# Second feed-forward product in halves of 256 columns, one PSUM bank each; both sums of the first product in one bank

## The chip, the cores and the metric

The kernel runs on one core of a Trainium2 chip. The metric is the device time of one execution in microseconds, median of several runs. The engines have one instruction queue each: TensorE (PE; its weight loads are listed apart as PEld), VectorE (DVE), ScalarE (ACT), GpSimd (POOL) and SyncE (SP, which issues the transfers). TensorE writes its results to PSUM, which has eight banks of 512 fp32 columns on 128 partitions; only ACT and DVE read them from there in this kernel.

## The reference

Windowed attention for 4 batches, 8 heads, 768 positions and a head width of 64, followed by a feed-forward layer on 3072 tokens of 512 values, with a hidden width of 2048:

```python
scores_l = scale * q @ k.T, kept where |i - j| < 16, else -1e9
scores_s = scale * q @ max_of_each_32_keys.T + log(32)
a = softmax(concat(scores_l, scores_s))
x = (a @ concat(v, mean_of_each_32_values))     # -> 3072 x 512 over all heads
h = x @ w_in                                    # 512 -> 2048
g = s * relu(h) ** 2 + b
return g @ w_out                                # 2048 -> 512, fp32
```

## The kernel before

The 3072 tokens are taken in 12 chunks `c` of `T = 256` tokens. For a chunk, attention runs in four units `p` of two heads, and leaves the chunk's `x` turned, 4 blocks `kc` of 128 values by 256 tokens. The feed-forward layer then goes over 16 blocks `f` of 128 hidden values.

- `hidden(c, f)` is the first product: tile `ph`, 128 hidden values by 256 tokens. From chunk 1 on, `x` and the weights are split in a rounded high part (`xh`, `wh`) and the rest (`xl`, `wl`), in the type fp32r, and three products of parts are summed: 3 terms by 4 blocks, 12 matmuls with 256 moving columns. Chunk 0 works in plain fp32 with 4 matmuls.
- `activate(c, f)` makes `g`: ACT takes relu out of PSUM (L371) and squares (L372), POOL multiplies and adds (L379), DVE rounds to `gh` (L381) and forms the rest `gl` (L383).
- `project(c, f)` is the second product: for each half `t` of the tokens, the three terms gl x wh, gh x wl, gh x wh with 512 moving columns of `w_out`, 6 matmuls (L398), summed over all 16 `f` in two tiles `po`.
- `evict(c)` copies the two `po` with ACT (L406) to SBUF and sends them out.

The order on each engine is written out by hand: `plan` holds functions under a step number, and they are called step by step, within a step by the order LOAD, SPLIT, ATT, WEIGHTS, HID, PE_ATT, CHAIN, PROJ, EVICT. Step `i = 16 c + f` has `activate(c, f)`. From chunk 1 on the matmuls go in pairs:

```python
at(i if c == 0 else i - i % 2, HID, hidden, c, f)
at(i, CHAIN, activate, c, f)
at(i + LAG if i + LAG < NF else (i + LAG) | 1, PROJ, project, c, f)
```

So TensorE's queue reads: hidden of an even and an odd block (24 matmuls), perhaps a piece of the next chunk's attention, project of the two blocks before (12 matmuls), and so on. The attention pieces are `transposes` (tile `pt`, four matmuls, turned probabilities), `values` (tile `pav`, 16 matmuls a unit) and `scores` (tiles `ps`, 16 matmuls a unit). From chunk 2 on, a chunk's hidden blocks 0 to 15 carry four `pt` pieces of one unit each, and two times `pav` and `ps` for two units together.

ACT's queue holds, between the two activations of a pair, what attention has for that step, and in chunk 1 also the roundings of the weights to `wh` (L143), two a step.

Eight PSUM banks are shared out by five pools: two for `po`, two for `ph`, two for `ps`, one for `pt`, one for `pav`. A framework puts a semaphore wait wherever an instruction writes or reads a tile that another engine still uses; two parts of one PSUM tile count as the same tile for this.

Of the kernel before, what the change touches and what calls it, by code (L numbers as in the profile page):

```python
# [10 lines left out]
F32 = mybir.dt.float32  # L11
# [7 lines left out]
P = 128  # L19
B, H, S, D = 4, 8, 768, 64  # L20
DM, DFF = 512, 2048
# [5 lines left out]
KR = WIN + NB  # L27
NSUB = 4
T = NSUB * SUB
# [5 lines left out]
NF = DFF // P  # L35
# [9 lines left out]
def windowed_attention_then_relu2_ffn(ctx, tc, qk, vwin, kt, vt, kq, vrow, wp, sb, out):  # L45


    nc = tc.nc
# [9 lines left out]
    ps_s = ctx.enter_context(tc.tile_pool(name="ps_s", bufs=2, space=bass.MemoryType.PSUM))  # L58
    ps_t = ctx.enter_context(tc.tile_pool(name="ps_t", bufs=1, space=bass.MemoryType.PSUM))
    ps_v = ctx.enter_context(tc.tile_pool(name="ps_v", bufs=1, space=bass.MemoryType.PSUM))  # L60

    ident = const.tile([P, P], F32, name="ident")
    sb_col = const.tile([P, 2], F32, name="sb_col")
# [132 lines left out]
    pm = []  # L196

    def mean_of_rows(n):
        if n == 0:
            pm.append(ps_po.tile([P, DM], F32, name="pm", tag="po"))  # L200
# [14 lines left out]
    qk_t, vw_t, ps_of, pr_of, mn_of, sm_of, pt_of, pT_of, o_of, xt = ({} for _ in range(10))  # L215
# [33 lines left out]
    def scores(c, p, j):  # L249
        q, kw = qk_t[c, p]  # L250
        if j == 0:
            if c == 0 and p % 2:
                both = [ps_h.tile([P, T], F32, name="ps", tag="ph") for _ in range(2)]
                ps_of[c, p] = [t[:, : 2 * KR].rearrange("p (j k) -> p j k", k=KR) for t in both]
            elif c < 2:
                ps_of[c, p] = [ps_s.tile([P, 4, KR], F32, name="ps", tag="ps") for _ in range(2)]
            elif p % 2 == 0:
                both = [ps_s.tile([P, 4, KR], F32, name="ps", tag="ps") for _ in range(2)]
                ps_of[c, p], ps_of[c, p + 1] = [t[:, :2] for t in both], [t[:, 2:] for t in both]
        for e in range(2):  # L260
            r = slice(64 * e, 64 * e + 64)
            for a in range(2):
                i = 2 * j + a
                o, qi = ps_of[c, p][e][64 * a : 64 * a + 64, j], q[r, i * SUB : (i + 1) * SUB]
                if c > 0:
                    nc.tensor.matmul(o, qi, kw[r, i, :], start=True, stop=True)  # L266
                    continue
                w = win_start(i)
                nc.tensor.matmul(o[:, :WIN], qi, kraw[0, p][r, w : w + WIN], start=True, stop=True)
                nc.tensor.matmul(o[:, WIN:], qi, ksum[0, p][r], start=True, stop=True)  # L270
# [38 lines left out]

    def transposes(c, p):  # L310
        pr = pr_of.pop((c, p))
        pt_of[c, p] = ps_t.tile([P, 4 * P], F32, name="pt")
        for n in range(4):
            nc.tensor.transpose(pt_of[c, p][:KR, n * P : (n + 1) * P], pr[:, n, :], ident)  # L314

# [7 lines left out]
    def values(c, p):  # L323
        vw, pT = vw_t.pop((c, p)), pT_of.pop((c, p))
        if c == 0 and p % 2:
            o_of[c, p] = ps_po.tile([P, DM], F32, name="pav", tag="po")
        elif c < 2 or p % 2 == 0:
            o_of[c, p] = ps_v.tile([P, 2 * T], F32, name="pav")
            if c > 1:
                o_of[c, p + 1] = o_of[c, p][:, T:]  # L330
        o = o_of[c, p]
        for i in range(NSUB):
            for e in range(2):
                nc.tensor.matmul(  # L334
                    o[64 * e : 64 * e + 64, i * SUB : (i + 1) * SUB],
                    vw[:, e, i, :], pT[:, e * T + i * SUB : e * T + (i + 1) * SUB], start=True, stop=True,
                )
# [11 lines left out]
            nc.vector.tensor_tensor(xt[c][1][:, kcs], o, xt[c][0][:, kcs].bitcast(F32), ALU.subtract)  # L349


    ph_of, gg, po = {}, {}, {}

    def hidden(c, f):
        ph = ph_of[c, f] = ps_h.tile([P, T], F32, name="ph", tag="ph")
        if c == 0:
            terms = [(w_f["in", f], xt[c][0], kc) for kc in range(NKC)]
        else:
            xh, xl = xt[c]
            terms = [  # L360
                (w["in", f], x, kc) for w, x in ((w_l, xh), (w_h, xl), (w_h, xh)) for kc in range(NKC)
            ]
        for n, (w, x, kc) in enumerate(terms):
            nc.tensor.matmul(  # L364
                ph, w[:, kc * P : (kc + 1) * P], x[:, kc], start=(n == 0), stop=(n == len(terms) - 1)
            )

    def activate(c, f):
        ph = ph_of.pop((c, f))
        r = p2.tile([P, T], F32, name="r")  # L370
        nc.scalar.activation(r, ph, AF.Relu)  # L371
        nc.scalar.activation(r, r, AF.Square)  # L372
        if c == 0:
            g = p2.tile([P, T], F32, name="g0", tag="gh", bufs=4)
            nc.vector.tensor_scalar(g, r, s_col, b_col, ALU.mult, ALU.add)  # L375
# [7 lines left out]
        nc.vector.tensor_tensor(gl, g, gh.bitcast(F32), ALU.subtract)  # L383
        gg[c, f] = gh, gl

    def project(c, f):
        if f == 0:
            for t in range(T // P):
                po[t] = ps_po.tile([P, DM], F32, name="po", tag="po")
        g = gg.pop((c, f))  # L390
        if c == 0:
            terms = [(g[0], w_f["out", f])]
        else:
            gh, gl = g
            terms = [(gl, w_h["out", f]), (gh, w_l["out", f]), (gh, w_h["out", f])]
        for t in range(T // P):
            for n, (a, w) in enumerate(terms):
                nc.tensor.matmul(  # L398
                    po[t], a[:, t * P : (t + 1) * P], w,
                    start=(f == 0 and n == 0), stop=(f == NF - 1 and n == len(terms) - 1),  # L400
                )

    def evict(c):
        for t in range(T // P):
            o = stage.tile([P, DM], F32, name="o", tag="stage")
            nc.scalar.copy(o, po[t])  # L406
# [86 lines left out]
    for i in range(NC * NF):  # L493
        c, f = divmod(i, NF)
# [65 lines left out]
```

## Time and profile before

| | us |
|---|---|
| median of 3 runs | 649.14 (648.83 to 649.5) |
| the profiled execution | 648.71 |
| its span in the profile | 647.0 |
| PE busy in the span | 628.1 (97%), 5164 matmuls and 5164 weight loads |
| DVE busy | 336.8 (52%) |
| ACT busy | 330.5 (51%) |
| POOL busy | 153.8 (24%) |
| mean granted TensorE clock | 0.999 |

How to read it: busy time counts overlapping matmuls once. The duration of a matmul row is modelled and longer than its share of the stream, since matmuls overlap, so the pace of TensorE is read from the starts of rows that follow each other, or from the chain of waits, which lists stretches of the critical engine one behind the other. A row "x24" in the chain is 24 instructions of that line. A row of the timeline begins with its start in us from the span's start and its length.

### The profile page before, as it was taken

How to read it: one execution, taken by the hardware profiler on the slowest of the kernel's cores; microseconds unless marked ns; L12 is line 12 of the kernel's file. 1: busy time of each engine (PE TensorE's matmuls, PEld its weight loads, DVE VectorE, ACT ScalarE, POOL GpSimd, SP SyncE). 2: the span in 40 equal slices, each digit the busy share in tenths (PEclk: the TensorE clock that was granted, in tenths of full speed). 3: DMA queues.
4: the chain of work that ended last, by engine and by line, in shares of the span. 5: the costliest groups of instructions: out<-in, count | busy, mean ns of one | idle time of the engine just before them, and what ended most of it. 6: DMA issues, size and time to landing. Idle time of an engine off the chain costs nothing.

```text
span 647.0 us, 13898 instructions
## 1 busy us (share of the span) xinstructions
PE 628.1 (97%) x5164; PEld 547.0 (85%) x5164; DVE 336.8 (52%) x1102; ACT 330.5 (51%) x972; POOL 153.8 (24%) x324
## 2 busy tenths in 40 slices
PE   6699999999999999999999999999999999999997
PEld 4456568989989899898999899898998989999996
DVE  6799998885443434356434434447443353342221
ACT  4898957845444435535435345444444444452322
POOL 3000004143133132232231331331322322312221
PEclk9999999999999999999999999999999999999999
DMA  9999405035203204134402301404410320100000
GB/s 329 388 382 352 128 2 186 2 102 191 72 1 104 72 2 131 57 82 145 138 1 62 115 2 36 152 22 135 145 65 2 105 72 2 57 3 1 33 2 33
DMA packets 25604, 63.25 MB, mean 98 GB/s; under 512 B 3968, under 2 KB 3968, under 8 KB 25536
## 3 DMA queue, kind: packets, MB, share of 16 engines
q1 hardware_dynamic: 25536, 62.36, 29.1%
q8 instruction: 41, 0.67, 0.4%
q14 instruction: 27, 0.22, 0.1%
HBM read 55.90 MB, written 6.29 MB: 96 GB/s over the span
## 4 chain that ended last, share of the span: by engine, by line
PE 86%; DVE 7%; DMA 5%; issue 0%; ACT 0%; SPq 0%; DVEq 0%
PE po L398 39%; PE ph L364 38%; PE pav L334 4%; PE ps L266 3%; PE pt L314 3%; DMA qk<-in_qk_dram 2%; DMA vw<-in_vwin_dram 1%; DMA wraw<-in_wp_dram 1%; DVE wf_out L134 1%; DVE wf_in L132 1%; DVE wf_out L132 1%; DMA kq<-in_kq_dram 1%; DVE wf_in L134 1%; DVE wf_in L130 1%; DVE wf_out L130 1%; DVE g L375 1%
## 5 line engine op out<-in xcount | busy, mean ns | idle before, releaser
L379 POOL TENSOR_SCALAR g<-r,sb_col 128x256 f32<-128x256 f32 x176 | 101.8, 578 | 418.5 <-ACT r L372 324.5
L381 DVE CAST gh<-g 128x256 fp32r<-128x256 f32 x176 | 52.3, 297 | 269.0 <-POOL g L379 268.6
L371 ACT ACTIVATE r<-ph 128x256 f32<-128x256 f32 x192 | 73.4, 382 | 210.1 <-PE ph L364 207.6
L398 PE MATMUL po<-wh,gl 128*128 128x512 f32 x352 | 143.2, 407 | 0.0
L398 PE MATMUL po<-wh,gh 128*128 128x512 f32 x352 | 138.6, 394 | 0.0
L398 PE MATMUL po<-wl_out,gh 128*128 128x512 f32 x352 | 137.7, 391 | 0.0
L364 PE MATMUL ph<-xh,wl_in 128*128 128x256 f32 x704 | 110.9, 280 | 0.0
L364 PE MATMUL ph<-xl,wh 128*128 128x256 f32 x704 | 108.7, 276 | 0.0
L364 PE MATMUL ph<-xh,wh 128*128 128x256 f32 x704 | 108.7, 276 | 0.0
L364 PEld LDWEIGHTS ph<-xh,wl_in 128*128 128x128 f32 x704 | 100.2, 188 | 8.2 <-issue 0.7
L364 PEld LDWEIGHTS ph<-xl,wh 128*128 128x128 f32 x704 | 93.8, 188 | 0.0
L364 PEld LDWEIGHTS ph<-xh,wh 128*128 128x128 f32 x704 | 92.9, 188 | 0.0
L372 ACT ACTIVATE r<-r 128x256 f32<-128x256 f32 x192 | 80.2, 418 | 6.1
L383 DVE TENSOR_TENSOR gl<-g,gh 128x256 fp32r<-128x256 f32 x176 | 76.4, 434 | 6.0
L398 PEld LDWEIGHTS po<-wh,gh 128*128 128x128 f32 x352 | 66.1, 188 | 14.3
L398 PEld LDWEIGHTS po<-wh,gl 128*128 128x128 f32 x352 | 66.2, 188 | 14.1 <-issue 3.0
L398 PEld LDWEIGHTS po<-wl_out,gh 128*128 128x128 f32 x352 | 66.3, 188 | 11.5
L298 ACT ACTIVATE pr<-pr,mn 128x120 f32<-128x120 f32 x176 | 67.3, 384 | 6.0 <-DVE mn L285 5.7
L321 ACT COPY pT<-pt 120x512 f32<-120x512 f32 x48 | 28.2, 587 | 35.8 <-PE pt L314 35.6
L364 PEld LDWEIGHTS ph<-x,wf_in 128*128 128x128 f32 x128 | 23.6, 190 | 17.3 <-issue 8.0
L244 POOL COPY vw<-vsum 24x256 f32<-24x256 f32 x80 | 36.7, 499 | 1.3
L364 PE MATMUL ph<-x,wf_in 128*128 128x256 f32 x128 | 31.0, 385 | 6.0 <-DVE wf_in L134 4.1
(70 smaller groups left out, 613.4 us busy)
## 6 DMA issues: line engine op xcount, KB each, us to landing
wraw<-in_wp_dram SPq DMA_DIRECT2D x32, 512.0 KB, 10.0
qk<-in_qk_dram SPq DMA_DIRECT2D x44, 368.0 KB, 4.7
vw<-in_vwin_dram SPq DMA_DIRECT2D x48, 192.0 KB, 4.6
out_dram<-o SPq DMA_DIRECT2D x24, 256.0 KB, 2.1
kraw<-in_kt_dram SPq DMA_DIRECT2D x12, 384.0 KB, 3.5
vraw<-in_vt_dram SPq DMA_DIRECT2D x12, 252.0 KB, 4.7
kq<-in_kq_dram SPq DMA_DIRECT2D x4, 512.0 KB, 4.6
vraw<-in_vt_dram SPq DMA_DIRECT2D x6, 264.0 KB, 6.5
```

Source lines behind the costliest of these rows:

```text
L244: filler(c).tensor_copy(vw_t[c, p][WIN:KR, e], vsum[bi][WIN : WIN + NB, 2 * p + e, :].unsqueeze(1).to_broadcast([NB, NSUB, D]),)
L266: nc.tensor.matmul(o, qi, kw[r, i, :], start=True, stop=True)
L298: nc.scalar.activation(pr, pr, AF.Exp, bias=mn_of[c, p][:, n : n + 1], scale=-1.0, accum_out=sm_of[c, p][:, n : n + 1])
L321: nc.scalar.copy(pT_of[c, p], pt_of.pop((c, p))[:KR])
L334: nc.tensor.matmul(o[64 * e : 64 * e + 64, i * SUB : (i + 1) * SUB], vw[:, e, i, :], pT[:, e * T + i * SUB : e * T + (i + 1) * SUB], start ...
L364: nc.tensor.matmul(ph, w[:, kc * P : (kc + 1) * P], x[:, kc], start=(n == 0), stop=(n == len(terms) - 1))
L371: nc.scalar.activation(r, ph, AF.Relu)
L372: nc.scalar.activation(r, r, AF.Square)
L379: nc.gpsimd.tensor_scalar(g, r, s_col, b_col, ALU.mult, ALU.add)
L381: nc.vector.tensor_copy(gh, g)
L383: nc.vector.tensor_tensor(gl, g, gh.bitcast(F32), ALU.subtract)
L398: nc.tensor.matmul(po[t], a[:, t * P : (t + 1) * P], w, start=(f == 0 and n == 0), stop=(f == NF - 1 and n == len(terms) - 1),)
```

## The change

The pools in PSUM go. Eight fixed tiles of one bank each take their place: `po0` to `po3` (`quarters`), `ph_bank`, `ps_a`, `ps_b` and `turn_bank` (named `pt`).

- `project` from chunk 1 on: each 512-column matmul becomes two of 256 columns with the same stationary operand. Token half `t` and column half `h` are summed in `quarters[2 * t + h]`, columns 0 to 255. Chunk 0 keeps 512 columns, in `quarters[0]` and `quarters[1]`.
- `evict` from chunk 1 on copies four tiles of 256 columns instead of two of 512; the transfers out stay.
- `hidden` from chunk 1 on writes an even block to the left half and an odd block to the right half of `ph_bank`. In chunk 0 odd blocks use `quarters[2]`.
- From chunk 2 on, turned probabilities (`pt`) and attended values (`pav`) share `turn_bank`; in chunks 0 and 1 the latter use `quarters[3]` (and `quarters[1]` for odd units of chunk 0).

```diff
-    ps_po = ctx.enter_context(tc.tile_pool(name="ps_po", bufs=2, space=bass.MemoryType.PSUM))
-    ps_h = ctx.enter_context(tc.tile_pool(name="ps_h", bufs=2, space=bass.MemoryType.PSUM))
...
+    quarters = [psum.tile([P, 512], F32, name=f"po{n}") for n in range(4)]
+    ph_bank, ps_a, ps_b, turn_bank = (psum.tile([P, 512], F32, name=n) for n in ("ph", "ps_a", "ps_b", "pt"))
...
     def transposes(c, p):
         pr = pr_of.pop((c, p))
-        pt_of[c, p] = ps_t.tile([P, 4 * P], F32, name="pt")
+        pt_of[c, p] = turn_bank
...
         if c == 0 and p % 2:
-            o_of[c, p] = ps_po.tile([P, DM], F32, name="pav", tag="po")
-        elif c < 2 or p % 2 == 0:
-            o_of[c, p] = ps_v.tile([P, 2 * T], F32, name="pav")
+            o_of[c, p] = quarters[1]
+        elif c < 2:
+            o_of[c, p] = quarters[3]
+        elif p % 2 == 0:
+            o_of[c, p] = turn_bank
...
+    def hidden_at(c, f):
+        return quarters[2][:, :T] if c == 0 and f % 2 else ph_bank[:, f % 2 * T : (f % 2 + 1) * T]
+
     def hidden(c, f):
-        ph = ph_of[c, f] = ps_h.tile([P, T], F32, name="ph", tag="ph")
+        ph = hidden_at(c, f)
...
         for t in range(T // P):
             for n, (a, w) in enumerate(terms):
-                nc.tensor.matmul(
-                    po[t], a[:, t * P : (t + 1) * P], w,
-                    start=(f == 0 and n == 0), stop=(f == NF - 1 and n == len(terms) - 1),
-                )
+                width = DM if c == 0 else DM // 2
+                for h in range(DM // width):
+                    nc.tensor.matmul(
+                        quarters[t if c == 0 else 2 * t + h][:, :width],
+                        a[:, t * P : (t + 1) * P], w[:, h * width : (h + 1) * width],
+                        start=(f == 0 and n == 0), stop=(f == NF - 1 and n == len(terms) - 1),
+                    )
 
     def evict(c):
         for t in range(T // P):
             o = stage.tile([P, DM], F32, name="o", tag="stage")
-            nc.scalar.copy(o, po[t])
+            if c == 0:
+                nc.scalar.copy(o, quarters[t])
+            else:
+                for h in range(2):
+                    nc.scalar.copy(o[:, h * T : (h + 1) * T], quarters[2 * t + h][:, :T])
```

TensorE's queue before, in the last chunk: hidden of blocks 14 and 15, then the first token half of project of block 12. In brackets stand the queues whose semaphores the first instruction of a row waits for.

```order
L364 MATMUL ph_8166<-xh_7448,wl_in_14_1620 128x256 [waits Activation_49]
L364 MATMUL ph_8166<-xh_7448,wl_in_14_1620 128x256 x3
L364 MATMUL ph_8166<-xl_7449,wh_14_1618 128x256 x4
L364 MATMUL ph_8166<-xh_7448,wh_14_1618 128x256 x4
L364 MATMUL ph_8179<-xh_7448,wl_in_15_1656 128x256 [waits Activation_49]
L364 MATMUL ph_8179<-xh_7448,wl_in_15_1656 128x256 x3
L364 MATMUL ph_8179<-xl_7449,wh_15_1654 128x256 x4
L364 MATMUL ph_8179<-xh_7448,wh_15_1654 128x256 x4
L398 MATMUL po_7872<-wh_12_1531,gl_8143 128x512 [waits DVE_49]
L398 MATMUL po_7872<-wl_out_12_1536,gh_8141 128x512
L398 MATMUL po_7872<-wh_12_1531,gh_8141 128x512
```

The same place now (`hidden` is L369, `project` L402):

```order
L369 MATMUL ph_80<-xh_8030,wl_in_14_1591 128x256 [waits Activation_49]
L369 MATMUL ph_80<-xh_8030,wl_in_14_1591 128x256 x3
L369 MATMUL ph_80<-xl_8031,wh_14_1589 128x256 x4
L369 MATMUL ph_80<-xh_8030,wh_14_1589 128x256 x4
L369 MATMUL ph_80<-xh_8030,wl_in_15_1639 128x256 x4
L369 MATMUL ph_80<-xl_8031,wh_15_1637 128x256 x4
L369 MATMUL ph_80<-xh_8030,wh_15_1637 128x256 x4
L402 MATMUL po0_76<-wh_12_1493,gl_8832 128x256 [waits DVE_49]
L402 MATMUL po1_77<-wh_12_1493,gl_8832 128x256
L402 MATMUL po0_76<-wl_out_12_1498,gh_8830 128x256
L402 MATMUL po1_77<-wl_out_12_1498,gh_8830 128x256
L402 MATMUL po0_76<-wh_12_1493,gh_8830 128x256
```

The second hidden block has no wait of its own any more, and the second product's matmuls go to two banks in turn, twice as many of half the width.

ACT's queue before, in chunk 1, the activations of blocks 8 and 9 (L371 relu, L372 square), with the roundings of weights and an exp of attention between:

```order
L371 ACTIVATE r_1518<-ph_1492 128x256 [waits PE_49,Pool_49]
L372 ACTIVATE r_1518<-r_1518 128x256 [waits Activation_49]
L143 CAST wh_12_1531<-wf_in_12_881 128x512
L143 CAST wh_12_1531<-wf_out_12_882 128x512
L298 ACTIVATE pr_1485,sums_1487<-pr_1485,mn_1486 128x120 [waits DVE_49] x2
L371 ACTIVATE r_1544<-ph_1505 128x256 [waits PE_49,Pool_49]
L372 ACTIVATE r_1544<-r_1544 128x256 [waits Activation_49]
```

The same place now (relu is L376, square L377):

```order
L376 ACTIVATE r_1480<-ph_80 128x256 [waits PE_49,Pool_49]
L377 ACTIVATE r_1480<-r_1480 128x256 [waits Activation_49]
L143 CAST wh_12_1493<-wf_in_12_836 128x512
L143 CAST wh_12_1493<-wf_out_12_837 128x512
L298 ACTIVATE pr_1449,sums_1451<-pr_1449,mn_1450 128x120 [waits DVE_49] x2
L376 ACTIVATE r_1506<-ph_80 128x256 [waits Pool_49]
L377 ACTIVATE r_1506<-r_1506 128x256 [waits Activation_49]
```

The order is the same. The second relu has no wait for TensorE of its own any more: both sums lie in one tile, and the first relu waits until both are written.

More of the change, by code (lines that the diff above doesn't have):

```diff
@@ L55, in windowed_attention_then_relu2_ffn @@
     p3 = ctx.enter_context(tc.tile_pool(name="p3", bufs=3))
-    ps_po = ctx.enter_context(tc.tile_pool(name="ps_po", bufs=2, space=bass.MemoryType.PSUM))
-    ps_h = ctx.enter_context(tc.tile_pool(name="ps_h", bufs=2, space=bass.MemoryType.PSUM))
-    ps_s = ctx.enter_context(tc.tile_pool(name="ps_s", bufs=2, space=bass.MemoryType.PSUM))
-    ps_t = ctx.enter_context(tc.tile_pool(name="ps_t", bufs=1, space=bass.MemoryType.PSUM))
-    ps_v = ctx.enter_context(tc.tile_pool(name="ps_v", bufs=1, space=bass.MemoryType.PSUM))
+    psum = ctx.enter_context(tc.tile_pool(name="psum", bufs=1, space=bass.MemoryType.PSUM))
+    quarters = [psum.tile([P, 512], F32, name=f"po{n}") for n in range(4)]
+    ph_bank, ps_a, ps_b, turn_bank = (psum.tile([P, 512], F32, name=n) for n in ("ph", "ps_a", "ps_b", "pt"))
     ident = const.tile([P, P], F32, name="ident")
@@ L199, in mean_of_rows @@
         if n == 0:
-            pm.append(ps_po.tile([P, DM], F32, name="pm", tag="po"))
+            pm.append(quarters[0])
         for j in (2 * n, 2 * n + 1):
@@ L252, in scores @@
             if c == 0 and p % 2:
[L253 to L259, printed above, removed]
+                ps_of[c, p] = [t[:, : 2 * KR].rearrange("p (j k) -> p j k", k=KR) for t in (ph_bank, quarters[2])]
+            else:
+                both = [t[:, : 4 * KR].rearrange("p (j k) -> p j k", k=KR) for t in (ps_a, ps_b)]
+                if c < 2:
+                    ps_of[c, p] = both
+                elif p % 2 == 0:
+                    ps_of[c, p], ps_of[c, p + 1] = [t[:, :2] for t in both], [t[:, 2:] for t in both]
         for e in range(2):
@@ L325, in values @@
         if c == 0 and p % 2:
-            o_of[c, p] = ps_po.tile([P, DM], F32, name="pav", tag="po")
-        elif c < 2 or p % 2 == 0:
-            o_of[c, p] = ps_v.tile([P, 2 * T], F32, name="pav")
+            o_of[c, p] = quarters[1]
+        elif c < 2:
+            o_of[c, p] = quarters[3]
+        elif p % 2 == 0:
+            o_of[c, p] = turn_bank
             if c > 1:
@@ L349, in attended @@
             nc.vector.tensor_tensor(xt[c][1][:, kcs], o, xt[c][0][:, kcs].bitcast(F32), ALU.subtract)
-    ph_of, gg, po = {}, {}, {}
+    gg = {}
+    def hidden_at(c, f):
+        return quarters[2][:, :T] if c == 0 and f % 2 else ph_bank[:, f % 2 * T : (f % 2 + 1) * T]
     def hidden(c, f):
-        ph = ph_of[c, f] = ps_h.tile([P, T], F32, name="ph", tag="ph")
+        ph = hidden_at(c, f)
         if c == 0:
@@ L368, in activate @@
     def activate(c, f):
-        ph = ph_of.pop((c, f))
+        ph = hidden_at(c, f)
         r = p2.tile([P, T], F32, name="r")
@@ L386, in project @@
     def project(c, f):
-        if f == 0:
-            for t in range(T // P):
-                po[t] = ps_po.tile([P, DM], F32, name="po", tag="po")
         g = gg.pop((c, f))
@@ L405, in evict @@
             o = stage.tile([P, DM], F32, name="o", tag="stage")
-            nc.scalar.copy(o, po[t])
+            if c == 0:
+                nc.scalar.copy(o, quarters[t])
+            else:
+                for h in range(2):
+                    nc.scalar.copy(o[:, h * T : (h + 1) * T], quarters[2 * t + h][:, :T])
             bi, ci = place(c)
```

## The prediction

> **What bounds the kernel now.** The page comes first: which engine is busy, at which clock, and what the chain of waits is made of.
>
> ```profile
> PE 628.1 (97%) x5164; PEld 547.0 (85%) x5164; DVE 336.8 (52%) x1102; ACT 330.5 (51%) x972; POOL 153.8 (24%) x324
> ...
> PE 86%; DVE 7%; DMA 5%; issue 0%; ACT 0%; SPq 0%; DVEq 0%
> PE po L398 39%; PE ph L364 38%; PE pav L334 4%; PE ps L266 3%; PE pt L314 3%; DMA qk<-in_qk_dram 2%; DMA vw<-in_vwin_dram 1%; DMA wraw<-in_wp_dram 1%; DVE wf_out L134 1%; DVE wf_in L132 1%; DVE wf_out L132 1%; DMA kq<-in_kq_dram 1%; DVE wf_in L134 1%; DVE wf_in L130 1%; DVE wf_out L130 1%; DVE g L375 1%
> ```
>
> TensorE is the bound, and the second product is the largest piece of its chain. The other engines are half idle. Next the chain in order of time, from chunk 10 to the end, shows whether TensorE ever waits.
>
> ```profile
> 567.41 1.08 PE pav L334 x32
> 568.50 0.98 PE ps L266 x32
> 569.48 2.95 PE po L398 x12
> 572.43 2.75 PE ph L364 x24
> ...
> 580.67 0.44 PE pt L314 x4
> 581.11 2.77 PE po L398 x12
> ...
> 602.11 2.75 PE ph L364 x24
> 604.86 2.75 PE po L398 x12
> 607.60 2.75 PE ph L364 x24
> ...
> 637.82 5.51 PE po L398 x24
> ...
> 643.35 0.59 ACT o L406
> ```
>
> Each piece starts where the last one ends: no wait. So from chunk 1 on the time is the number of matmuls by their pace, and the change is weighed by pace. 12 wide matmuls take 2.74 to 2.75 us, 228.8 ns each; 24 narrow ones take 2.75 us, 114.6 ns each. Halving a wide one would then change nothing, so the pace inside a group has to be read: the timeline of the last groups.
>
> ```profile
> 634.67 0.39 PE L398 MATMUL po<-wh,gh 128*128 128x512 f32 x1
> 634.90 0.64 PE L364 MATMUL ph<-xh,wl_in 128*128 128x256 f32 x4
> ...
> 636.29 0.62 PE L364 MATMUL ph<-xh,wl_in 128*128 128x256 f32 x4
> ...
> 637.65 0.39 PE L398 MATMUL po<-wh,gl 128*128 128x512 f32 x1
> ```
>
> The first 12 narrow matmuls behind wide ones take 1.39 us, the next 12 take 1.36 us, 113.3 ns each. Narrow matmuls run a little faster than half a wide one, but start slowly behind wide ones.
>
> **The change part by part.**
>
> *Halves instead of whole matmuls.* The first of the three terms of the second product, from chunk 1 on:
>
> ```profile
> L398 PE MATMUL po<-wh,gl 128*128 128x512 f32 x352 | 143.2, 407 | 0.0
> ```
>
> Three terms of 352 are 1056 wide matmuls, 88 groups of 12; they become 2112 narrow ones. Their stationary operand stands twice in a row, but it is loaded twice: where this kernel already uses one operand for two matmuls, each line has its own loads.
>
> ```profile
> L269 PEld LDWEIGHTS ps<-kq x64: 129/156/228, 4.7 to 13.2; 64*64 64x64 f32 x64
> ...
> L270 PEld LDWEIGHTS ps<-ksum,kq x64: 133/155/228, 5.7 to 13.4; 64*64 64x64 f32 x64
> ```
>
> A half is then the same kind of instruction as one of the first product: fp32r, 128x128 stationary, 256 moving columns, its own load. Its price is the settled 113.3 ns: 226.6 for two against 228.8, so 1056 x 2.2 ns = **2.3 us less**. The bounds are the slowest and the fastest pace of 256 columns in the trace, below: 118.0 ns (two cost 236.0: 7.6 us more) and 108 ns a pass (216: 13.5 us less). I take 113.3, since the instruction's form is the same and nearly all of the first product settles there. Issue is no limit: `pav` and `ps` above put 64 matmuls with their loads into 2.06 us, 32 ns each.
>
> *Slow starts.* A first-product group pays 2.745 - 24 x 0.1133 = 0.025 us for starting behind wide matmuls. There are 88 such groups, and the width no longer changes in front of them: 2.2 us less if the start goes, 0 if it stays. But of the 88 second-product groups 60 follow fp32 pieces of attention (attention of chunks 2 to 11, each with four `pt` and two `pav`/`ps` pieces: 10 x 6), and a narrow group behind fp32 may start slowly too: 60 x 0.025 = 1.5 us more. I take both: **0.7 us less**.
>
> *Both sums in one bank.* The relu of the even block now waits for the odd block's last matmul, one group of 12 later, about 1.36 us; behind it in ACT's queue stand its square, attention's exps or copies, in chunk 1 the roundings to `wh`, and the second relu. TensorE's next first-product matmul waits for that second relu, where before it waited for the first one only. Chunk 2 shows the ordinary case, chunk 1 the crowded one.
>
> ```profile
> 171.56 0.39 ACT L371 ACTIVATE r<-ph 128x256 f32<-128x256 f32 x1 [2.20 <-PE ph L364]
> ...
> 173.06 0.36 ACT L371 ACTIVATE r<-ph 128x256 f32<-128x256 f32 x1
> ...
> 175.41 0.64 PE L364 MATMUL ph<-xh,wl_in 128*128 128x256 f32 x4
> ```
>
> Here the second relu ends at 173.42; 1.36 later is 174.78, and TensorE needs the bank at 175.41: 0.63 us spare. In pairs with `pt` or `pav` TensorE comes later still.
>
> ```profile
> 121.27 0.39 ACT L371 ACTIVATE r<-ph 128x256 f32<-128x256 f32 x1 [1.49 <-PE ph L364]
> ...
> 123.81 0.36 ACT L371 ACTIVATE r<-ph 128x256 f32<-128x256 f32 x1
> ...
> 125.12 0.64 PE L364 MATMUL ph<-xh,wl_in 128*128 128x256 f32 x4
> ```
>
> In chunk 1 (blocks 8 and 9) the second relu would end at 124.17 + 1.36 = 125.53, and TensorE wants the bank at 125.12: 0.41 us late. With the like at chunk 1's first pair (its ACT queue is as full) I take **0.6 us more**; bounds 0 and 1.6 (0.2 for each of its 8 pairs). The Trainium skill (PSUM — Partial Sum Buffer, section on PSUM bank collisions) says that two engines may not touch one bank and quadrant at once, whatever the columns; so ACT could not read the left half earlier. No run here shows such a collision; guarded by columns instead of by bank, this term would be 0 and the sum 0.6 lower.
>
> The longer road to `g` is covered except, nearly, at the last pair:
>
> ```profile
> 636.55 0.39 ACT L371 ACTIVATE r<-ph 128x256 f32<-128x256 f32 x1 [3.30 <-PE ph L364]
> ...
> 638.47 0.43 DVE L383 TENSOR_TENSOR gl<-g,gh 128x256 fp32r<-128x256 f32 x1
> ...
> 640.40 0.39 PE L398 MATMUL po<-wh,gl 128*128 128x512 f32 x1
> ```
>
> From relu to `gl` takes 638.90 - 636.55 = 2.35 us; begun 1.36 later it ends at 640.26, 0.14 before TensorE uses it. Other pairs have a first-product pair more in between.
>
> *Eviction.* Copies of 256 columns cost 362 ns, of 512 columns 588.
>
> ```profile
> L406 ACT COPY o<-po 128x512 f32<-128x512 f32 x24 | 14.1, 588 | 17.4 <-PE po L398 15.3 <-DVE vhalf L175 1.3
> L347 ACT COPY x<-pav 128x256 f32<-128x256 f32 x4 | 1.4, 362 | 1.8 <-PE pav L334 1.8
> ```
>
> Four instead of two cost ACT 0.27 us a chunk, hidden ten times: the banks are needed again a pair later. At the very end the first two of the four still run when the last matmul ends: **0.1 us more**. Attended values and `pt` in one bank cost nothing: `pav` needs the copied `pt` anyway, and the next `pt` comes four steps after `pav`. Chunk 0's widths stay.
>
> Sum: -2.3 - 0.7 + 0.6 + 0.1 = -2.3 us. The profiled execution's 648.71 (span 647.0 and 1.7 around it) becomes 646.4; it lies 0.4 under the median of 649.14, which becomes 646.8. I forecast 646.7.
>
> **The rivals.** Two of them rest on these rows.
>
> ```profile
> 90.27 1.89 PE L364 MATMUL ph<-x,wf_in 128*128 128x256 f32 x8
> 92.00 1.88 PE L398 MATMUL po<-wf_out,g 128*128 128x512 f32 x4
> ...
> 94.19 0.64 PE L364 MATMUL ph<-xl,wh 128*128 128x256 f32 x4
> ...
> 96.55 3.60 PE L398 MATMUL po<-wf_out,g 128*128 128x512 f32 x8
> 99.58 1.03 PE L364 MATMUL ph<-xh,wl_in 128*128 128x256 f32 x4
> 100.45 0.62 PE L364 MATMUL ph<-xl,wh 128*128 128x256 f32 x4
> ...
> 101.36 0.62 PE L364 MATMUL ph<-xh,wl_in 128*128 128x256 f32 x4
> ```
>
> 1. *A slow rhythm* (slower). From 94.19 to 96.55 twenty narrow fp32r matmuls take 2.36 us, 118.0 ns each: the only group that never settles, and it stands behind fp32 work, as 60 second-product groups will. If all 60 pairs ran so, 60 x 48 x 4.7 ns = 13.5 us come on top, less the 1.5 already counted: 658.7. It decides against the change from about 10 pairs of 60. Against it: the group at 99.58, also behind fp32, settles (100.45 to 101.36: eight in 0.91 us, 113.8 ns each). How many pairs would be caught, no row tells; one in ten costs 1.2 us.
> 2. *A fixed price for each matmul* (slower). In fp32, 90.27 to 92.00 is 216 ns for 256 columns, and 96.55 to 99.58, less 0.03 of overlap at its end, 429 ns for 512: two halves cost 3 ns more than the whole. By that, 1056 x 3 = 3.2 us more, with 0.7 for waits and the end: 653.0. Against it: the fp32r rows say -2.2 instead. The Trainium skill (TensorE: Matmul & The Clock Gate, section Back-to-back issue gap) has this rule, columns over 2.4 GHz plus about 2.5 ns: by it a split costs about 2.5 ns more; this trace agrees in fp32, and not in fp32r, where 512 columns take 228.8.
> 3. *No gain*. The halves run at just half of 228.8, the slow starts stay, and the 0.7 remain: 649.8.
> 4. *More gain*. Alternating banks or a repeated operand let a half run at fp32's pace of 108 ns a pass: 13.5 us less, slow starts aside: 636. No fp32r row is that fast.
>
> **How the numbers follow.** The forecast has 0.62, with a range of its own from 644.6 (no waits, no slow starts) to 647.7 (waits at their bound); rival 1 has 0.10, rival 2 0.06, rival 3 0.14, rival 4 0.08. The range of 644.0 to 651.0 holds the forecast, rival 3 and cases of rival 1 with up to 20 of the 60 pairs, about 0.8; its lower end lies 0.6 under the forecast's own, for halves at 113.0 ns. Within 0.2% (1.3 us, about what a measurement can tell) lies rival 3 in most of its spread, and the forecast's upper edge: 0.13. Faster: 0.59 of the forecast and rival 4, 0.67. Slower: rivals 1 and 2 and the rest of rival 3, 0.20.
>
> **What would show it.** In the chain, second-product groups of 24 at 2.72 us, 2.74 behind attention, and first-product groups of 24 at 2.72 instead of 2.75; one or two breaks by ACT's relu between 95 and 130 us; 5164 + 1056 = 6220 matmuls and as many loads; four copies of about 0.37 at the end. The forecast is wrong if groups of 24 at 2.83 appear (rival 1), if both kinds stay at 2.75 (rival 3), or if relu stands in the chain in later chunks.

## The result: slower, 655.1 against the 646.7 forecast

After the change: 655.12 us (median of 4 runs, 654.75 to 655.60), before it 649.05 on the same chip; ratio 1.0087, 95% interval 1.0075 to 1.0099. The forecast had said 646.7, within 644.0 to 651.0: wrong in sign.

The page of the changed kernel (span 653.0, profiled execution 654.75) still names TensorE, with the number of matmuls forecast:

```profile
PE 633.5 (97%) x6220; PEld 596.4 (91%) x6220; DVE 337.2 (52%) x1102; ACT 325.3 (50%) x994; POOL 160.2 (25%) x324
...
PE 86%; DVE 7%; DMA 5%; ACT 1%; issue 0%; SPq 0%; ACTq 0%; DVEq 0%
```

No new bound, and 5.4 us more of TensorE's own busy time. The chain of waits over the last chunk (start, length, piece) shows where:

```profile
597.75 1.08 PE pt L336 x32
598.83 3.02 PE po L402 x24
601.85 2.83 PE ph L369 x24
604.68 2.83 PE po L402 x24
607.51 2.73 PE ph L369 x24
610.24 2.72 PE po L402 x24
612.96 2.83 PE ph L369 x24
615.79 2.83 PE po L402 x24
618.62 2.73 PE ph L369 x24
621.35 2.72 PE po L402 x24
...
643.58 2.72 PE po L402 x24
...
646.32 3.00 PE po L402 x23
```

Two lengths alternate, for both products: 2.72 us (113.4 ns a matmul) and 2.83 us (117.9 ns), with nothing between the pieces. The rhythm turns over where a first-product group (`ph`) follows a second-product group (`po`), and is kept from `ph` to `po`. By the starts of all matmul rows from 90 us on, it turns over at 84 of the 86 steps from `po` to `ph` and stays at all 27 from `ph` to `po`; behind a piece of attention 41 of 60 `po` groups are slow. In all, 42 of 88 first-product groups and 46 of 88 second-product groups are slow; before, one of 88 first-product groups was. 88 groups at 0.105 us are 9.2 us: without them the time would be 645.9, near the forecast.

The wait at the shared bank is in the chain, at blocks 8 and 9 of chunk 1:

```profile
120.33 2.75 PE ph L369 x24
...
123.16 0.40 ACT r L376
...
123.58 0.42 ACT r L377
124.00 1.03 ACT wh L143 x2
125.03 0.77 ACT pr L298 x4
125.81 0.28 ACT r L376
...
126.12 3.01 PE ph L369 x24
```

Both sums are written at 123.1; the second relu comes behind the first, its square, two roundings to `wh` and exps, and TensorE waits for it: 0.50 us, by the 612 ns between the two matmul starts instead of 114. At the first pair of chunk 1 the wait costs nothing: it delays one matmul by 0.12 us (147 ns after the start of chunk 0's last one instead of 28), and the one behind it starts 547 ns after chunk 0's last, against 546 in the kernel before.

### The profile page after: what moved, and what is told of

Same layout as the page of the kernel before. It is cut to its first block, busy times and chain, and to the rows that moved or that the text cites. A ratio compares the mean times of both kernels' runs of the same rounds, so it can differ in the third digit from the quotient of the medians.

```text
span 653.0 us, 15951 instructions
## 1 busy us (share of the span) xinstructions
PE 633.5 (97%) x6220; PEld 596.4 (91%) x6220; DVE 337.2 (52%) x1102; ACT 325.3 (50%) x994; POOL 160.2 (25%) x324
## 4 chain that ended last, share of the span: by engine, by line
PE 86%; DVE 7%; DMA 5%; ACT 1%; issue 0%; SPq 0%; ACTq 0%; DVEq 0%
PE po L402 39%; PE ph L369 38%; PE pt L336 3%; PE ps_a L266 3%; PE pt L314 3%; DMA qk<-in_qk_dram 2%; DMA vw<-in_vwin_dram 1%; DMA wraw<-in_wp_dram 1%; DVE wf_out L134 1%; DVE wf_out L132 1%; DVE wf_in L132 1%; DMA kq<-in_kq_dram 1%; DVE wf_in L134 1%; DVE wf_in L130 1%; DVE wf_out L130 1%; DVE g L380 1%
## 5 line engine op out<-in xcount | busy, mean ns | idle before, releaser
L376 ACT ACTIVATE r<-ph 128x256 f32<-128x256 f32 x184 | 70.2, 381 | 272.7 <-PE ph L369 267.0
L402 PE MATMUL po<-wh,gl 128*128 128x256 f32 x704 | 144.2, 286 | 0.0
L402 PE MATMUL po<-wl_out,gh 128*128 128x256 f32 x704 | 138.6, 278 | 0.0
L402 PE MATMUL po<-wh,gh 128*128 128x256 f32 x704 | 138.4, 278 | 0.0
L369 PE MATMUL ph<-xh,wl_in 128*128 128x256 f32 x704 | 111.4, 280 | 0.3 <-ACT r L376 0.3
L369 PE MATMUL ph<-xh,wh 128*128 128x256 f32 x704 | 110.1, 279 | 0.0
L369 PE MATMUL ph<-xl,wh 128*128 128x256 f32 x704 | 110.0, 278 | 0.0
L402 PEld LDWEIGHTS po<-wh,gl 128*128 128x128 f32 x704 | 106.7, 188 | 3.3 <-DVE gh L386 3.0
L402 PEld LDWEIGHTS po<-wh,gh 128*128 128x128 f32 x704 | 106.7, 187 | 0.0
L402 PEld LDWEIGHTS po<-wl_out,gh 128*128 128x128 f32 x704 | 106.7, 188 | 0.0
L369 PEld LDWEIGHTS ph<-xh,wl_in 128*128 128x128 f32 x704 | 95.1, 188 | 1.5 <-ACT r L376 0.9
L369 PEld LDWEIGHTS ph<-xh,wh 128*128 128x128 f32 x704 | 94.0, 188 | 0.0
L369 PEld LDWEIGHTS ph<-xl,wh 128*128 128x128 f32 x704 | 94.0, 188 | 0.0
L377 ACT ACTIVATE r<-r 128x256 f32<-128x256 f32 x192 | 80.4, 419 | 6.1
L244 POOL COPY vw<-vsum 24x256 f32<-24x256 f32 x80 | 41.9, 564 | 1.3
L308 DVE TENSOR_TENSOR pr<-pr,rs 128x480 f32<-128x480 f32 x48 | 35.2, 734 | 1.7
L298 ACT ACTIVATION_READ_ACCUMULATOR pr<-pr,mn 128x1 f32 x176 | 33.4, 190 | 0.0
L402 PE MATMUL po<-wf_out,g 128*128 128x512 f32 x64 | 30.4, 601 | 0.0
```

Source lines behind the costliest of these rows:

```text
L244: filler(c).tensor_copy(vw_t[c, p][WIN:KR, e], vsum[bi][WIN : WIN + NB, 2 * p + e, :].unsqueeze(1).to_broadcast([NB, NSUB, D]),)
L298: nc.scalar.activation(pr, pr, AF.Exp, bias=mn_of[c, p][:, n : n + 1], scale=-1.0, accum_out=sm_of[c, p][:, n : n + 1])
L308: nc.vector.tensor_tensor(pr, pr, rs.unsqueeze(2).to_broadcast([P, 4, KR]), ALU.mult)
L369: nc.tensor.matmul(ph, w[:, kc * P : (kc + 1) * P], x[:, kc], start=(n == 0), stop=(n == len(terms) - 1))
L402: nc.tensor.matmul(quarters[t if c == 0 else 2 * t + h][:, :width], a[:, t * P : (t + 1) * P], w[:, h * width : (h + 1) * width], start=(f ...
```

## The experiments

In each, "slow" counts groups of 24 narrow matmuls near 117.9 ns, of 88 in each product.

**e1, the banks without the halves.** 512 columns everywhere, in the first two of the four tiles, and evicted so; the other banks as changed.

```diff
-                width = DM if c == 0 else DM // 2
+                width = DM
```

> The new share of the banks alone: the second product keeps 512 columns. Theory A (narrow matmuls fall into a slow rhythm of 118 ns, the banks only cost the two waits seen in chunk 1): 649.05 + 0.6 = 649.7 us, every first-product group of 24 at 2.75 us as before, no second-product group changed. Theory B (the shared bank is what makes groups slow): about 652 to 655, with first-product groups of 2.83.

Measured 650.84 against 649.55, ratio 1.0020 (1.0010 to 1.0030); 1 slow first-product group, as before. The banks cost about 1.3 us (0.6 to 2.0), not 6; in the trace chunk 1 takes 0.58 us longer and the chunks behind it, at 50.29 us, do not.

**e2, the halves without the banks.** `project` writes column halves of the two old tiles; the first and the last matmul of each sum stay wide.

```diff
+                opens, closes = f == 0 and n == 0, f == NF - 1 and n == len(terms) - 1
+                width = DM if c == 0 or opens or closes else DM // 2
...
+                        po[t][:, h * width : (h + 1) * width],
```

> Halves of 256 columns in the banks of before: both column halves of a token half in one bank, the first product in two banks, eviction by 512 columns. The first and the last matmul of each sum over f stay 512 wide (44 of 1056). Theory A: slow groups stay, only the waits of 0.6 go: 654.5 us, first-product groups of 2.73 and 2.83 mixed. Theory B (the shared bank, or the alternation of banks from matmul to matmul): groups of 2.72 throughout and about 646 us.

653.73 against 649.55, 1.0060 (1.0045 to 1.0075): 27 slow first-product groups, more than 50 slow second-product groups. The slow rhythm comes with the halves, not with the new banks.

**e3, one half behind the other.** The loop over `h` outside that over `n`, so that operand and bank change less often.

> The change with the column half as the outer loop and the three terms inside: no stationary operand stands twice in a row any more (but for gh, whose two terms follow each other), and the bank changes every third matmul instead of every one. Theory A: the slow groups stay, 655 us within 2. Theory C (the operand loaded twice in a row, or the bank changed at every matmul, sets the slow rhythm): 646 us with all groups at 2.72 to 2.75.

654.91, 1.0076 (1.0058 to 1.0093), with the counts of the changed kernel (42 and 46 slow). A repeated operand or alternating banks aren't the cause.

**e4, bare streams.** First- and second-product groups on constant tiles, with no other engine.

> Leaves out the whole computation: only streams of fp32r matmuls on TensorE, without any wait between them, each stream behind wide matmuls and four fp32 transposes. Streams: pairs of first-product groups (24) and second-product groups (24 narrow) as in the changed kernel; the same with the first product in two banks; with both halves in one bank; half by half; only first-product groups; only second-product groups; with transposes between. Theory A: each stream runs group by group at either 113 or 118 ns a matmul, 2.72 or 2.83 us for 24, and the rhythm turns over at the step from a second-product to a first-product group also without waits. If the waits turn it over, every stream here keeps one rhythm from its sixth matmul on. If it is the banks, the streams with two banks or one bank run at 113 throughout.

Neither rhythm appeared, but a third one, in every stream:

```profile
37.16 0.44 PE b L94 x4
37.60 2.87 PE b L74 x24
40.47 2.88 PE b L90 x24
```

120.0 ns a matmul, and no turnover. Something that the kernel has was missing here.

**e5 and e6, some wide matmuls left in.** From e2, the last matmul of each second-product group wide (e5), or the first and the last (e6).

```diff
-                width = DM if c == 0 or opens or closes else DM // 2
+                whole = c == 0 or opens or closes or (t == 1 and n == 2)
+                width = DM if whole else DM // 2
```

> The kernel with halves in the old banks (653.73 beside 649.55), with the last matmul of each second-product group, gh x wh of the second token half, kept 512 columns wide: one wide matmul stands directly ahead of each of the 88 first-product groups, 22 halves stand before it. Theory A' (a group's rhythm is set by what stands directly ahead of it, and a wide matmul there gives the fast one): first-product groups 88 fast and none slow instead of 61 and 27, so 27 x 0.105 = 2.8 us less than with halves alone, 650.9. Theory D (the rhythm is turned over by the number of narrow matmuls or by the waits at a group's start, whatever stands ahead): still 20 to 40 slow first-product groups, 653 to 655. Second-product groups stay as they were by both, about half of them slow.

> As the kernel before it in this call, and the first matmul of each second-product group, gl x wh of the first token half, is kept wide too: 2 wide ones around 20 halves. Theory A': a wide matmul directly ahead sets the fast rhythm for the halves as well, also behind attention; nearly no slow group is left, and every group of 24 costs what a first-product group behind wide ones costs before, 2.745 us: the time of the kernel before, 649.5 (648.5 to 650.0). A'' (one wide matmul isn't enough behind fp32 pieces): the 20 halves behind attention run at 118 ns in some 50 groups, 50 x 20 x 4.6 ns = 4.6 us more, 654 less 2.8 for fast first-product groups, 651. Theory D: 653 to 655.

659.10 (1.0153, 1.0136 to 1.0170) and 657.53 (1.0127, 1.0111 to 1.0142), with 58 and 64 slow first-product groups. My theory of a wide matmul that resets the rhythm fell.

**e7, waits, other engines and sizes in the streams.**

> Leaves out the whole computation: streams of narrow fp32r matmuls in groups of 24 as in the kernel, as in the bare streams that ran at 120.0 ns, now with one thing added in each stretch: ACT reads the first product's bank, so that the next first-product group waits for it (W1); DVE writes gl anew, so that the second-product groups wait for it (W2); both; other engines busy with copies that TensorE has nothing to do with (O); all. Then moving operands of 288, 320 and 384 columns, stationary operands of 96 and 64 columns, and a single wide matmul ahead of every 24, 12 and 4 narrow ones. Theory W (a wait, though long fulfilled, shifts load against matmul and so sets the rhythm): W1 or W2 brings 113.4 or 117.9 ns in some groups, O alone leaves 120.0. Theory O (reads of SBUF by other engines set it): O alone leaves 120.0 for another pace. Theory L (load and matmul are about equally long and take turns in setting the pace): with 64 stationary columns the rhythms are gone, one pace below 113; from 320 columns on one pace of about columns times 0.42 plus 10 to 15 ns, 146 at 320 and 173 at 384; rival: 120/256 for each column, 150 and 180. A single wide matmul ahead: by A' the narrow ones start at 113 to 114.

With waits, with busy engines, with both: 120.0 ns throughout, so both theories fell, and a single wide matmul ahead left 120.0 too. With 64 stationary columns, whose load row is 134 ns long instead of 188, the pace was 113.3; 320 and 384 moving columns took 146.7 and 173.3. So the load has a part in the pace of a 256-column matmul, but that doesn't tell why the kernel is faster than the stream.

**e8, where the operands start.** In the compiled programs the operands of the streams all start at a multiple of 128 bytes in SBUF. In the kernels they don't. The traces hold no addresses; the table has them from the compiled programs, in bytes counted from 128 bytes beyond a multiple of 256 (so 0 and 128 are multiples of 128):

```
                        first product          second product
                     stationary  moving      stationary  moving
before, changed       w   0      x 192       gh, gl 192    w 0
e9                    w   0      x 0, 128    gh, gl 0, 128 w 0
e10, e12, e13         w   0      x 192       gh, gl  64    w 0
e11                   w   0      x 192       gh, gl   0    w 0
e16, e17, e18         w  64      x   0       gh, gl  64    w 0
```

> Leaves out the whole computation: streams of 36 narrow fp32r matmuls, with the start of the stationary and of the moving operand in SBUF moved by 0, 32, 64 and 96 bytes (all 16 pairs), and a few by 128 and 256; then groups of 24 that alternate between two pairs. In the streams that ran at 120.0 ns all operands started at multiples of 128 bytes. In the kernels xh and xl (moving) start 64 bytes off such a multiple and wh, wl (stationary) on one; in the second product gh and gl (stationary) start 64 bytes off, the weights (moving) on one. Theory S (where the operands start sets the pace): equal starts 120.0 ns again; starts 64 bytes apart 113.4 or 117.9 ns; 128 and 256 change nothing; the alternation of (stationary 0, moving 64) with (64, 0) turns over between 113.4 and 117.9 as in the changed kernel, and the same pair all the time does not. Rival (starts do nothing): 120.0 ns in every stretch, no turnover.

Chain pieces of the streams of 36 (L100; the other lines separate them), the starts running through stationary 0, 32, 64 and for each moving 0, 32, 64, 96:

```profile
34.89 4.31 PE b L100 x36
...
43.74 4.21 PE b L100 x36
...
52.49 4.24 PE b L100 x36
...
61.29 4.31 PE b L100 x36
...
105.33 4.11 PE b L100 x36
...
193.47 4.10 PE b L100 x36
...
202.12 4.24 PE b L100 x36
```

The first four are (stationary, moving) = (0, 0), (0, 32), (0, 64), (0, 96), the next (64, 0), the last two (128, 64) and (256, 64). The settled pace in ns, from the starts of their last 12 matmuls:

```
stationary   moving 0    32     64     96
     0        120.0   116.7  117.8  120.0
    32        118.1   120.0  116.7  117.8
    64        113.3   118.5  120.0  116.7
    96        119.0   117.8  118.3  120.0
```

Equal starts give 120.0; (0, 128) and (0, 256) too. I had expected that 128 bytes more change nothing, but (0, 64) runs at 117.8, (128, 64) at 113.3 and (256, 64) at 117.8 again: here 128 bytes matter, and 256 don't. The two kinds of group in turn, and each alone:

```profile
210.91 27.79 PE b L100 x240
...
243.24 22.62 PE b L100 x192
...
270.41 21.79 PE b L100 x192
```

Groups of 24 with (0, 64) and (64, 0) in turn average 115.8 ns and go 117.8, 113.3, 113.3, 117.8, 117.8, 113.3 ns, the changed kernel's very pattern, with no wait and no other engine. (0, 64) alone stays at 117.8, (64, 0) alone at 113.3. Moving less stationary start, modulo 256 bytes, is 64 for (0, 64) and 192 for (64, 0); in the kernel it is 192 in the first product and 64 in the second. So the seam is the same too: in both the rhythm turns over where a 192 group follows a 64 group, and stays the other way round. The difference alone isn't all, since (96, 32) also has 192 and ran at 117.8.

**e9, the stream's starts in the kernel.** `xh`, `xl`, `gh` and `gl` moved by 64 bytes.

```diff
-        gh = p2.tile([P, T], F32R, name="gh", tag="gh", bufs=4)
+        gh = p2.tile([P, 32 + T], F32R, name="gh", tag="gh", bufs=4)[:, 16 : 16 + T]
```

> The changed kernel, with xh, xl, gh and gl moved by 64 bytes in SBUF, so that every operand of both products starts at a multiple of 128 bytes, as in the bare streams. Theory S: all 176 groups of both products run at 120.0 ns, 2.88 us each, none at 113.4 or 117.9: 176 x 2.88 = 506.9 us instead of the 504.5 measured after the change, 657.5 in all. Rival (starts do nothing): about half of the groups fast and half slow as in the changed kernel, 655.1.

666.41, 1.0271 (1.0254 to 1.0288): no fast group left, as theory S said, but the groups settle between 118 and 120 ns and not all at 120.0.

```profile
612.55 2.85 PE ph L374 x24
615.40 2.83 PE po L407 x24
618.23 2.84 PE ph L374 x24
621.06 2.85 PE po L407 x24
```

2.84 us instead of 2.88, and a larger rise than the 657.5 expected: I had set 506.9 against 504.5, which holds other matmuls and waits; 88 groups of 2.83 and 88 of 2.72 are 488.4, and 176 of 2.84 are 11.4 more, as measured.

**e10 to e13, one kind of difference for both products.** Pads of 128 bytes (e11: 64) ahead of `gh` and `gl`.

```diff
+            if f == 0:
+                pad("pad0", 32)
             g = p2.tile([P, T], F32, name="g0", tag="gh", bufs=4)
```

> The changed kernel, with gh and gl moved by 128 bytes in SBUF (two pads; nothing else moves by other than a multiple of 256). Where the moving operand starts, less where the stationary one starts, modulo 256 bytes: 192 in the first product (x 64, weights 128), 64 in the second (weights 128, gh and gl 64). In the streams 192 settled at 113.3 ns by itself, 64 stayed at 117.8, 0 and 128 ran at 120.0, and the rhythm turned over each time a 192 group followed a 64 group. The move makes the second product 192 too. Theory S: no group follows one of another kind, no turnover, and groups behind attention settle at 113.3 within some 6 matmuls: 88 slow groups gone, 88 x 0.105 = 9.2 us less than 655.1, 645.9, below the kernel before. Rival S' (what counts is that the tiles change, not where they start): half of the groups slow as now, 655. Rival S'' (the slow rhythm, once taken up behind attention, then stays): up to 176 slow groups, 664.

> The kernel before, 512 columns, with gh and gl moved by 64 bytes: the difference of starts in the second product becomes 0 (before: 64). In the streams wide matmuls with difference 0 settled at 226.7 ns; here they take 228.8. Theory S: 1056 x 2.1 = 2.2 us less, 647.0, if first-product groups behind them still settle at 113.3. Rival (wide matmuls don't depend on it): no change, 649.2.

> The kernel before, 512 columns, with gh and gl moved by 128 bytes: the difference of starts in the second product becomes 192. In the streams wide matmuls with 192 took 230 and 236 in turn, 233.6 ns. Theory S: 1056 x 4.8 = 5.1 us more, 654.3; more if first-product groups don't settle behind them (88 x 0.105 = 9.2 on top). Rival: no change, 649.2.

> Halves in the old banks (column halves of the two wide tiles; first and last matmul of each sum wide), with gh and gl moved by 128 bytes. Theory S: the slow groups go as with the new banks, and the 0.6 us of waits for the shared bank too: 645.3, 0.3 more for the 44 wide ones at 233.6: 645.6. Rival S': 653.7, as without the move.

e10: 655.70, 1.0095 (1.0081 to 1.0109). Behind attention the second-product groups are now fast (59 of 60), but the rhythm turns at other places, and 61 first-product and 27 second-product groups are slow: 88 again. The 645.9 of theory S is missed.

```profile
599.75 2.93 PE po L413 x24
602.68 2.83 PE ph L369 x24
605.51 2.83 PE po L413 x24
608.34 2.74 PE ph L369 x24
611.08 2.83 PE po L413 x24
613.90 2.74 PE ph L369 x24
```

So the starts decide in the kernel too, but the difference between moving and stationary start isn't the whole rule. e13 agrees (655.50, 1.0096, 1.0081 to 1.0112; expected 645.6). e12: 654.40 (1.0077, 1.0064 to 1.0089), near the 654.3 expected, but by luck: the wide groups, at 2.79 to 2.80, add some 3.4 us and not 5.1, and 25 slow first-product groups the rest. e11 is the surprise: 654.72 (1.0079, 1.0065 to 1.0092) instead of 647.0. The wide matmuls sped up to 226.7 ns, but behind them 87 of 88 first-product groups are slow:

```profile
605.63 2.72 PE po L409 x12
608.35 2.83 PE ph L364 x24
611.18 2.72 PE po L409 x12
613.89 2.83 PE ph L364 x24
```

**e14 and e15, 64 pairs of starts.**

> Leaves out the whole computation: for each of 64 pairs (X, G), three pairs of a first-product group (24 narrow; stationary 0, moving X bytes beyond a multiple of 256 plus 128) and a second-product group in halves (24 narrow; stationary G, moving 0), behind four turns. X and G run through 0, 32 to 224 bytes; only x, gh and gl would have to be moved for any of them. The changed kernel is X = 192, G = 192, the moved one X = 192, G = 64. Theory S2 (a load runs beside the matmul before it, so at the seam between two groups the new stationary start meets the old moving one, and there the rhythm can turn over): turnover at (192, 192) and at (192, 64), mean pace 115 to 116.5; 119 to 120.0 at (0, 0); some pairs hold 113.3 to 113.8 in both groups. Rival (two kinds of operands always turn it over): no pair below 115.

> The same grid with second-product groups of 12 wide matmuls instead of 24 halves. The kernel before is X = 192, G = 192: wide 228.8 and narrow 114.6 on the mean, 2.75 us a group each; X = 192 with G = 0 (e11's start is G = 0 or 128 by the same measure) narrow ones at 117.9, wide ones at 226.7; X = 192 with G = 64 wide ones at 233. Theory S2: some pairs have both, narrow at 113.3 to 113.8 and wide at 226.7: 5.44 us for both groups instead of 5.49. Rival: none is under 5.47.

With halves no pair holds the fast rhythm in both groups: on the mean of the second and third repeat, a first- and a second-product group together take 5.55 us at best, 5.56 at the changed kernel's starts, 5.76 at worst. So the 113.3 to 113.8 in both that was expected of some pairs did not come. With wide matmuls the starts of the kernel before are the best of the 64, 5.49 us; the next takes 5.53. For halves that leaves the same starts in both products, for which the weights must move too.

**e16 and e17, the same starts in both products.**

```diff
-            pair = slots.tile([P, 2, 512], F32R, name=f"wh_{key[1]}", tag="slot")
-            w_h["in", key[1]], w_h["out", key[1]] = pair[:, 0], pair[:, 1]
+            pair = slots.tile([P, 1088], F32R, name=f"wh_{key[1]}", tag="slot")
+            w_h["in", key[1]], w_h["out", key[1]] = pair[:, 16:528], pair[:, 576:1088]
...
-    stage = ctx.enter_context(tc.tile_pool(name="stage", bufs=4))
+    stage = ctx.enter_context(tc.tile_pool(name="stage", bufs=3))
```

> The changed kernel with the same starts in both products: w_in (high part and rest), gh and gl moved so that every stationary operand starts 64 bytes, and x so that every moving one starts 0 bytes beyond a multiple of 256 plus 128; in the stream that held this pair all the time, every group of 24 took 2.720 us. The room for it comes from one buffer less of qk and of the staging tiles, and the ring of weights is cut into one for w_in and one for w_out; the order of work stays. Theory S2 (the rhythm turns over at the seam between operands with other starts): no seam is left, no turnover, also behind attention a group settles at 113.3 ns: 88 slow groups of 0.105 us go, 9.2 us less than 655.1, less 1 us or so for settling behind attention and for later loads: 645.5 to 647.5, below the kernel before (649.2). Rival (a turnover comes with any change of tile, or of bank, in the kernel): half of the groups stay slow, 655.

> The same starts, with the halves in the old banks (column halves of the two wide tiles, first and last matmul of each sum wide; two banks for the first product's sums). Theory S2: as the kernel beside it, less the 0.6 us of waits for the shared bank, plus 0.2 for the 44 wide ones: 645.0 to 647.2. Rival: 653.7, as the halves in the old banks were.

e16: 4 first-product and 2 second-product groups slow, and yet 656.72 (1.0112, 1.0092 to 1.0132). The timeline at 305 us shows why: idle time and its releaser in brackets.

```profile
304.74 0.65 ACT L436 COPY o<-po 128x256 f32<-128x256 f32 x2 [2.06 <-DVE vhalf L182]
...
306.46 0.39 PE L423 MATMUL po<-wh,gh 128*128 128x256 f32 x2
309.21 0.65 ACT L436 COPY o<-po 128x256 f32<-128x256 f32 x2 [3.83 <-DMA out_dram<-o]
309.64 0.66 PE L423 MATMUL po<-wh,gl 128*128 128x256 f32 x2 [2.79 <-ACT o L436]
```

The copies out of `po` wait for a staging tile, the one that I had taken away, and TensorE for the copies; the like stands at 154 and 461 us, the loads of each batch. Behind the long gap at 306.6 us the granted clock falls as well (0.76 from 309.6 to 312 us, 0.72 to 316), and narrow matmuls start 213 ns apart from 310.9 us on: this chunk lost 4.9 us, the two others with such a wait 2.4 each. e17 (657.39, 1.0139, 1.0117 to 1.0161) has the same room and 25 slow first-product groups again. But for one group behind chunk 0's fp32 work, each stretch of slow groups begins at a second-product group that holds a wide matmul, at a chunk's first or last block: equal starts alone don't keep the rhythm. Its banks differ from e16's too, so that the widths alone turn it over is likely, not shown.

**e18, the staging tile given back.** `g` is formed in place in `r`'s tile, and one tile of the mean values goes.

```diff
-        g = p2.tile([P, T], F32, name="g")
+        g = r
```

> As e16, the same starts in both products, but with all four staging tiles again; the room comes from one buffer less of qk, from multiplying and adding in place (g in the tile of r) and from one tile of the mean values less. In e16 a chunk without a long wait took 49.90 us, before the change 50.30 and after it 50.73; four chunks of e16 had waits of 0.4 to 4.9 us for gl and for the bank. Theory (those waits came from the missing staging tile, at the loads of the next batch): they go, ten chunks gain 0.40 us each against the kernel before, chunk 1 loses 0.4: 3 us less, 646.1 (645.5 to 647.0), a gain. Rival (the waits come from what both kernels lack, a buffer of qk, or from the new tiles' order): some of them stay, 649 to 657.

647.07 us against 649.81, ratio 0.9959 (0.9947 to 0.9970): faster than both kernels, though by 0.4% only. One slow group of the 176 is left, at 100 us behind chunk 0's fp32 work.

```profile
PE 627.1 (97%) x6220; PEld 589.2 (91%) x6220; DVE 336.2 (52%) x1102; ACT 324.7 (50%) x994; POOL 158.0 (24%) x324
```

TensorE's busy time on its page is 6.4 us below the changed kernel's, and its chain in the last chunk is even:

```profile
594.48 2.72 PE ph L379 x24
597.20 2.72 PE po L416 x24
599.92 2.72 PE ph L379 x24
602.64 2.72 PE po L416 x24
...
635.28 5.62 PE po L416 x47
```

From chunk 5's first matmul to chunk 6's it takes 49.93 us, the changed kernel 50.73, the kernel before 50.29. It still has the 0.5 us wait at 125 us.

## Why the prediction was wrong, step by step

- *Halves instead of whole matmuls: the step that failed.* The price of 113.3 ns was that of "the same kind of instruction" in the first product, and "nearly all of the first product settles there". But the form doesn't fix the pace. The first product settles there because of where its operands start (e9 moves them, and no group settles at 113.3) and because of what stands ahead (e11 moves only `gh` and `gl`, and 87 of 88 first-product groups no longer settle). The second product's operands start elsewhere; with halves on both sides of the seam the rhythm turns over there, and half of all groups run at 117.9. That is 9.2 us more than the term allowed: 46 x 0.105 = 4.8 in the second product, and 4.4 in the first, which the term took as unchanged.
- *Rival 1, the slow rhythm,* had the right pace (118.0 from the row at 94.19) and nearly the right price (4.7 ns a matmul, 0.11 us a group, against 0.105), and its sign, groups of 24 at 2.83, is what the chain shows; but it had a chance of only 0.10. Its trigger, fp32 work ahead, is half of the matter: 41 of the 60 second-product groups behind attention are slow (none of them in e18, with other starts), but the turnover at the step from `po` to `ph` comes without fp32 work, in the bare stream too (e8), and makes 40 of the slow first-product groups.
- *Rival 2, a fixed price,* forecast 653.0, and that this lies nearer to 655.1 than the forecast is luck: two halves cost 226.6 or 235.8 ns, not the wide one's 228.8 and a fixed 3. By the rule that the Trainium skill gives for a matmul by itself (TensorE: Matmul & The Clock Gate, section Back-to-back issue gap), an estimate for 256 columns is 109.2 ns. No fp32r row of the two kernels agrees, with 113.3 and 117.9; nor is there one at rival 4's 108. With equal starts the runs show 120.0, 146.7 and 173.3 ns at 256, 320 and 384 columns: 13.3 ns and 0.417 ns a column.
- *Slow starts.* Where all groups are fast, the start of a first-product group costs some 5 ns (2.724 us in e18 against 24 x 113.3 ns), as assumed. Behind `pt` a second-product group takes 2.74 to 2.75 us there, the 0.025 that was counted; but a wide group paid most of that already (2.77 at 581.11 against 2.75), so the 1.5 us more was mostly not new.
- *Both sums in one bank.* Forecast 0.6 from two waits of chunk 1; the trace shows 0.50 for one, and nothing for the first pair. e1 puts all of the banks at 0.6 to 2.0.
- *The last pair.* Forecast 0.14 us to spare; the gap of 295 ns between two matmul starts at 646.0, instead of 114, shows a wait of 0.18. Most of the difference is the road from relu to the end of `gl`: 2.59 us (643.68 to 646.27) instead of 2.35, since that `gl` took 0.67 us and not 0.43. The rest of that stream is slow.
- *Eviction* stayed hidden, but for what e16 took away. At the very end 0.1 us more was forecast; from the end of the last matmul to the end of the span it takes 3.63 us, 3.69 before.
- *The sum.* Where the rhythm holds (e18) the gain is 2.7 us, near the 2.3 forecast. The mechanism that was priced exists, and needs starts that the change didn't bring. That the moved starts, and not the small changes that made room, bring it rests on the counts of slow groups (88 to 1, and to 6 in e16 with other small changes) and on a chunk's 0.8 us; no run has the small changes alone.

## What to carry to other kernels

A price taken from "the same instruction elsewhere in the trace" holds only for its operands' places and its neighbours; where a trace shows two paces for one form, as here at 94.19 us, find what selects them before choosing one. Before splitting matmuls to 256 columns, compare where the stationary and moving operands start, and make neighbouring groups alike; moving a tile by 64 bytes is a cheap trial. When room is taken from one pool for a trial, look for the wait that this brings before judging the trial.

## What the runs showed of the hardware

- Of fp32r matmuls with 128 stationary and 256 moving columns, each with its load, one form has paces from 113.3 to 120.0 ns (6%), set by where the two operands start in SBUF, and a history: with the starts (0, 64) both 117.8 and 113.3 can last for a whole group (e8). The stationary start counts beyond 128 bytes: beside a moving start of 64 it gives 117.8 at 0, 113.3 at 128 and 117.8 at 256. In the trace of the changed kernel a load starts some 3 ns after the matmul ahead of it in both rhythms, and its own matmul 110 ns (fast) or 114 to 115 ns (slow) after that.
- Wide ones move too: 226.7 (e11), 228.8 (before) and 233 ns (e12), by 64 and 128 bytes.
- The Trainium skill (SBUF — State Buffer, section Who interferes with whom) gives TensorE two independent read ports, for the moving operand and for loads. The runs don't show which part of the chip couples the two, only that the pace depends on both starts together; what it is stays open, and so does why one pair of starts has two lasting rhythms.
